# Order of the weight loads in one DMA queue, and place of the last row sums, in a fused attention and soft-MoE kernel

## The chip, the cores and the metric

The kernel runs on one core of one Trainium2 chip. The metric is the device time of one execution in microseconds (us); smaller is better. Times of a profile count from the start of its span.

## The reference

Two stages follow each other. Attention has 4 batches, 8 heads, 768 positions and head dimension 64. Four of the heads ("retrieval") see all earlier positions, the other four only the first 4 positions and a window of 64. Its output is turned into 3072 rows of 512 numbers, the input `x` of a soft mixture of experts with 8 experts of 4 slots:

```python
logits = x @ phi                       # 3072 x 32
d = softmax over the rows of logits    # dispatch, per slot
slot_input = d.T @ x                   # 32 x 512
slot_out[e] = relu(slot_input[e] @ w1[e]) @ w2[e]   # w1: 512 x 1024, w2: 1024 x 512
out = softmax over the slots of logits @ slot_out   # 3072 x 512
```

All inputs and the output are float32 in HBM.

## The kernel before, in words

**Loads.** All large inputs come through one queue, POOL's, which casts float32 to bfloat16 on the way: q, k and v in "quads" of four heads of a batch (8 quads each, `load`, L100), 8 first expert matrices `w1s` and 8 second ones `w2s` (`w_load`, L389 to L394; the last ones in halves of 256 columns, `w2_half`, L396). The order is that of the string `LOADS` (L39): its first six entries are issued at the start, the rest by `issue` (L492), called after each `turn` of a quad. A name such as `v7` may go out only when the quad two before it (`v5`) has been turned, since it is put in the same buffer; a `w` is the next expert matrix and has no such condition. But the list is taken strictly in order, and POOL issues in order. What is left of the first 12 matrices after the list goes out behind the turn of `v6` (`weights(12)`, L521). The buffers of q, k and v and of the masks are those of `w2s[4]` to `w2s[7]`, so these matrices come last: (4), (5) and the first half of (6) behind the last turn of `v7` (L523 to L525), the other three halves (7,0), (6,1), (7,1) after the attention's last mask (L578).

A DMA further waits for the eighth one before it on the same queue: the trace shows POOL's issues from 65.45 us on ended by landings of such loads.

**Attention.** The instruction order of TensorE (PE), ScalarE (ACT) and VectorE (DVE) is written out by hand in `ORDER` (L41): `Tv7.1` turns half of v's quad 7 on PE (L120), `ev7.1` copies it out of PSUM, `Q` are scores (L166), `x` exponentials (L174), `M` masks (L193), `P` the products with v (L208), `N` the division (L220, L222), `X`, `L`, `S`, `B`, `D` the logits, their exponentials and the slot inputs of a finished batch. Each engine runs its part strictly in this order, so PE at a `T` whose quad has not landed holds up all that follows.

**Around the end of the attention.** `expT` holds the exponentials of the logits, one block a batch. `row_sums(b)` (L598) makes the sums over slots of one batch, six matmuls of one column each. For batches 0 to 2 they run ahead of the last slot inputs; for the last batch, at L620, they wait for ScalarE's copy of the last exponentials (`last_turn`, L297). One reciprocal of all 24 sums follows on DVE (L621, `rrow`).

**Experts.** `first(e4, c)` (L637) makes half the hidden units of four experts (16 matmuls of 512 columns into one PSUM bank), `turn_h` transposes them, `second(es, cols)` (L658) multiplies with w2. The expert banks 0 to 7 lie where the attention's PSUM pools were: scores in 0 to 3, two tiles in turn; the tile `tail` in 4 and 5; transposes in 6 and 7. The last two experts come per half of the columns (L729, L733): `slot_out` columns 0 to 255 need halves (6,0) and (7,0), columns 256 to 511 need (6,1) and (7,1).

**Output.** For eight of twelve blocks of 256 rows, the first half of the columns is made and stored as soon as the first half of `slot_out` is there (`half_rows(i, 0)`, 8 stores of 256 KB), then the second half (8 more), then the other four blocks whole (`full_rows`, 4 stores of 512 KB). All 20 stores go through SP's queue in this order (L691). PE, DVE and ACT only feed them.

Of the kernel before, what the change touches and what calls it, by code (L numbers as in the profile page):

```python
# [35 lines left out]

LOADS = "q0 k0 v0 q1 k1 v1 q2 k2 v2 w q3 k3 w v3 q4 k4 w v4 w q5 k5 v5 w q6 k6 w v6 q7 k7 w w v7 w".split()  # L39

ORDER = """  # L41
Tq0.0 Tq0.1 E eq0.0 eq0.1 Y4 Tk0.1 H2.3 H1.2 Tk0.0 H1.1 ek0.1A H0.1 H0.0 ek0.0 H0.2 H0.3 Y4 Q0.1 H1.3 Q0.4
# [31 lines left out]
HP = [0, 1, 2, 3, 4, 5, 6, 7]  # L74
# [255 lines left out]
def kernel(  # L330
# [13 lines left out]
    nc = tc.nc  # L344
    P = 128
    B, H, S, D = q.shape
# [12 lines left out]
    for i, t in enumerate("qkv"):  # L359
        w = w2s[4 + i].rearrange("p f (hp c) -> p (f hp c)", hp=2)  # L360
# [7 lines left out]
    quarter = singles.tile([P, 1], BF16, name="quarter")  # L368
# [3 lines left out]
    rrow = singles.tile([P, B, 6], F32, name="rrow")  # L372
# [115 lines left out]

    queue = LOADS[6:]
    turns = {}  # L490
# [86 lines left out]
    bl = B - 1  # L577
# [4 lines left out]
    tail = unread[0]  # L582
    sip = tail[:, 0, :4 * ES].rearrange("p (o s) -> p o s", o=4)

    def slot_inputs(x, first):
        v = x.rearrange("p (di do) -> p do di", do=4)
        if first:
            nc.tensor.matmul(tail[:, 0, :4 * ES], ident, zero[:, :4 * ES], start=True, stop=False)
        for do in range(4):
            nc.tensor.matmul(sip[:, do, :], v[:, do, :], sum4, start=False,  # L590
                             stop=not first and do == 3)

    def out_rows(b, c, r):
        return expT[:, b, 256 * c + r:256 * c + 256:2]

    rp = tail[:, 1, 448:448 + 6 * B].rearrange("p (b c) -> p b c", b=B)

    def row_sums(b):  # L598
        for c in range(3):
            for r in range(2):  # L600
                nc.tensor.matmul(rp[:, b, 2 * c + r:2 * c + r + 1], out_rows(b, c, r), quarter, start=True, stop=True)

    slot_inputs(slot_sa, True)
    fill(2)
# [3 lines left out]
    at.by_feature(nc.scalar.copy, slot_sl, slice(0, 256), slps[0])  # L608
    at.by_feature(nc.vector.tensor_copy, slot_sl, slice(256, 512), slps[1])
    at.last_exps(bl, True)  # L610
    for b in range(bl):
        row_sums(b)
    slot_inputs(slot_sl, False)
    nc.vector.tensor_copy(siT, sip)
    at.last_turn(bl)
# [1 line left out]
    nc.vector.reduce_sum(csum, colpart, axis=AX.X)  # L617
    rcol = singles.tile([P, 1], F32, name="rcol")
    nc.vector.reciprocal(rcol, csum)
    row_sums(bl)  # L620
    nc.vector.reciprocal(rrow, rp)  # L621
    sctx.close()
    mlp = ctx.enter_context(tc.tile_pool(name="mlp", bufs=2, reuse_waits="tile"))
    osb = ctx.enter_context(tc.tile_pool(name="osb", bufs=12, reuse_waits="tile"))
# [2 lines left out]
    def bank(i, shape, dt=F32):  # L627

        return tps.tile(shape, dt, tag=f"b{i}", name=f"b{i}")
# [7 lines left out]
    def first(e4, c):  # L637
        hp = bank(HP[2 * e4 + c], [P, 512])
        for do in range(4):
            for g in range(4):  # L640
                nc.tensor.matmul(hp[32 * g:32 * (g + 1), :], siT[:, do, :], w1s[4 * e4 + g][:, do, c * 512:(c + 1) * 512],
                                 start=(do == 0), stop=(do == 3))
        if e4 not in hss:
            hss[e4] = mlp.tile([P, 2, 512], BF16, tag="hs", name="hs")
        if c == 0:
            nc.scalar.activation(hss[e4][:, 0], hp, ACT.Relu, scale=emask[:, e4:e4 + 1])
        else:
            nc.vector.tensor_scalar(hss[e4][:, 1], hp, emask[:, e4:e4 + 1], 0.0, op0=ALU.mult, op1=ALU.max)

    def turn_h(e4):  # L650
        tp = bank(HP[4 + e4], [P, 8, P], BF16)
        hv = hss[e4].rearrange("p c f -> p (c f)").rearrange("p (fi fo) -> p fo fi", fo=8)
        for fo in range(8):
            nc.tensor.transpose(tp[:, fo, :], hv[:, fo, :], ident)
        hTs[e4] = mlp.tile([P, 8, P], BF16, tag="hT", name="hT")
        nc.vector.tensor_copy(hTs[e4], tp)
# [15 lines left out]

    first(0, 0)
    first(0, 1)
    first(1, 0)
    turn_h(0)
    first(1, 1)
# [96 lines left out]
```

## Time and profile before

| | |
|---|---|
| time, median of 3 runs | 150.86 us (150.58 to 151.81) |
| the profiled execution | 151.69 us, of which its span 149.9 us |
| busy in the span | PE 124.4, weight loads into PE 83.1, DVE 113.2, ACT 103.8, POOL 35.3 us |
| PE's granted clock, mean | 0.948 |
| HBM read, written | 52.50 MB, 6.29 MB |
| DMA packets | 16838, 32.91 MB |

The span is what the profiler covers; 1.8 us of the profiled execution lie around it. The profile's second part cuts the span in 40 slices of 3.75 us, with a digit for the busy tenths of each engine. An "idle before" in a timeline is the time in which an engine waited ahead of an instruction, with what ended the wait. A DMA has an issue time and a time to landing; the sum of both is when its data can be used. Both are told per load, by the window of its issue.

### The profile page before, as it was taken

The numbers are of one execution on the slowest core, as the hardware profiler recorded it, in microseconds if no ns is written. First come the engines' busy times: TensorE is split into PE (matmuls) and PEld (weight loads), VectorE is DVE, ScalarE is ACT, GpSimd is POOL, SyncE is SP. The second block draws the span as 40 slices with busy tenths as digits, with TensorE's granted clock in tenths as the row PEclk, the third lists the DMA queues.
The fourth block names the chain that finished last, engine by engine and source line by source line (L and its number), as shares of the span: only waits on it lengthen the run. The fifth ranks groups of instructions, "written<-read, shape, count | busy, mean of one in ns | idle before, by whom it ended". The sixth has DMA issues, their size and how long they took to land.

```text
span 149.9 us, 5211 instructions
## 1 busy us (share of the span) xinstructions
PE 124.4 (83%) x2301; PEld 83.1 (55%) x2303; DVE 113.2 (76%) x256; ACT 103.8 (69%) x142; POOL 35.3 (24%) x68
## 2 busy tenths in 40 slices
PE   6899999999999999999999947989879699575000
PEld 2455677677766676658657725556556457451000
DVE  4898999999969999998999973488993343758000
ACT  3049899999899999889989962289931430769000
POOL 6634401603146022337220000064033000000000
PEclk9999999999999999999999995599999999999855
DMA  2999999999999999999999999999999999789995
GB/s 22 197 210 210 211 234 202 215 230 192 227 207 219 204 210 222 207 220 218 199 229 212 211 221 213 214 223 210 214 219 214 192 198 196 159 301 346 345 405 201
DMA packets 16838, 32.91 MB, mean 220 GB/s; under 512 B 1712, under 2 KB 9904, under 8 KB 15024
## 3 DMA queue, kind: packets, MB, share of 16 engines
q0 software_dynamic: 11168, 26.22, 91.3%
q1 hardware_dynamic: 5648, 6.37, 12.4%
q8 instruction: 18, 0.29, 0.7%
q14 instruction: 4, 0.03, 0.1%
HBM read 52.50 MB, written 6.29 MB: 392 GB/s over the span
## 4 chain that ended last, share of the span: by engine, by line
PE 28%; DMA 25%; issue 21%; ACT 11%; POOL 4%; DVE 2%; ACTq 0%; POOLq 0%
DMA w<-in_q_dram 13%; DMA w<-in_moe_w_dram 12%; PE sc L166 8%; PE pv L208 6%; ACT pT L174 6%; PE tpk L120 2%; PE tpv L120 2%; ACT ot L711 2%; PE tpx L231 2%; PE tpq L120 2%; POOL w L397 1%; POOL expT L264 1%; PE tpb L138 1%; PE zp L422 1%; ACT ot L724 1%
## 5 line engine op out<-in xcount | busy, mean ns | idle before, releaser
L174 ACT ACTIVATE pT<-sc 128x1024 bf16<-128x1024 f32 (+1 forms) x96 | 81.3, 930 | 9.3 <-PE sc L166 9.0
L193 DVE TENSOR_TENSOR pT<-pT,w 128x1024 bf16<-128x1024 bf16 (+2 forms) x64 | 32.6, 524 | 3.1 <-ACT pT L174 3.0
L166 PE MATMUL sc<-qT,kT 64*128 64x512 bf16 (+3 forms) x256 | 33.0, 313 | 1.9 <-ACT pT L174 1.3
L208 PEld LDWEIGHTS <-pT 128*128 128x128 bf16 x672 | 25.5, 99 | 9.9 <-issue 7.9
L208 PE MATMUL pv<-vb,pT 128*128 128x65 bf16 x352 | 28.9, 196 | 0.1
L120 PEld LDWEIGHTS <-w 96*64 96x64 bf16 x768 | 18.9, 111 | 12.3 <-issue 6.2
L208 PE MATMUL pv<-vf,pT 128*128 128x65 bf16 x320 | 24.7, 196 | 0.0
L222 DVE TENSOR_TENSOR xb<-pv,rs 128x768 bf16<-128x768 f32 (+1 forms) x17 | 15.5, 910 | 0.6
L166 PEld LDWEIGHTS <-kT 64*128 64x128 bf16 x256 | 10.3, 94 | 9.8 <-issue 3.9
L264 POOL COPY expT<-ep 128x128 bf16<-128x128 bf16 x18 | 6.8, 426 | 22.8 <-ACT ep L260 22.6
L120 PE MATMUL tpv<-ident,w 96*64 96x96 bf16 x256 | 8.6, 213 | 3.1 <-DMA w<-in_v_dram 3.1
L153 DVE TENSOR_TENSOR vf<-vb,fmask 128x528 bf16<-128x528 bf16 x16 | 11.2, 697 | 0.0
L711 ACT ACTIVATE ot<-b,rrow 128x256 f32<-128x256 f32 x16 | 6.0, 489 | 6.9 <-PE b L705 6.9
L132 DVE COPY vT<-tpv 128x768 bf16<-128x768 bf16 x14 | 7.4, 548 | 3.1 <-PE tpv L120 3.1
L236 DVE COPY xT<-tpx 128x768 bf16<-128x768 bf16 x16 | 8.7, 549 | 1.1 <-PE tpx L231 1.1
L103 POOL DMA_DIRECT2D w<-in_k_dram x8 | 5.1, 641 | 17.7 <-PE sc L166 11.6
L231 PE MATMUL tpx<-ident,xb 128*128 128x128 bf16 x96 | 8.3, 224 | 1.0 <-DVE xb L222 0.8
L120 PE MATMUL tpq<-ident,w 96*64 96x96 bf16 x256 | 8.1, 209 | 0.7 <-DMA w<-in_q_dram 0.7
L132 DVE COPY qT<-tpq 128x768 bf16<-128x768 bf16 x15 | 8.0, 548 | 0.6 <-PE tpq L120 0.6
L422 PE MATMUL zp<-w 128*128 128x512 bf16 x21 | 7.3, 480 | 1.3 <-DVE quarter L425 1.2
L120 PE MATMUL tpk<-ident,w 96*64 96x96 bf16 x256 | 8.3, 209 | 0.0
L103 POOL DMA_DIRECT2D w<-in_q_dram x8 | 5.3, 667 | 12.1 <-PE tpq L120 11.2
(106 smaller groups left out, 149.3 us busy)
## 6 DMA issues: line engine op xcount, KB each, us to landing
w<-in_moe_w_dram POOLq DMA_DIRECT2D x14, 1024.0 KB, 21.6
out_dram<-ot SPq DMA_DIRECT2D x16, 256.0 KB, 3.5
w<-in_q_dram POOLq DMA_DIRECT2D x8, 384.0 KB, 15.1
w<-in_k_dram POOLq DMA_DIRECT2D x8, 384.0 KB, 13.8
w<-in_v_dram POOLq DMA_DIRECT2D x8, 384.0 KB, 18.1
w<-in_moe_w_dram POOLq DMA_DIRECT2D x4, 512.0 KB, 17.1
out_dram<-ot SPq DMA_DIRECT2D x4, 512.0 KB, 4.6
phf<-in_moe_phi_dram SPq DMA_DIRECT2D x4, 16.0 KB, 9.3
```

The costliest lines, as they stand in the source:

```text
L103: self.nc.gpsimd.dma_start(self.raws[t][Q % 2][:96], s)
L120: self.nc.tensor.transpose(tp[64 * hp:64 * hp + 64, x, :], raw[:96, hp, s * 64:s * 64 + 64], self.ident[:96, :96])
L132: self.nc.vector.tensor_copy(o, i)
L153: self.nc.vector.tensor_mul(vf, self.vbs[n // 2 % 2][:, n % 2, :, :4, :], fm.to_broadcast([128, 2, 4, VW]))
L166: nc.tensor.matmul(sc[:, hh, o:o + w], kT[ps, (g0 + j) * 128:(g0 + j + 1) * 128], qT[ps, g0 * 128 + q0:g0 * 128 + q0 + w], start=True, sto ...
L174: self.nc.scalar.activation(self.pT[n][:, :, lo:hi], self.sc.pop((n, u))[:, :, :hi - lo], ACT.Exp, scale=self.scale)
L193: nc.vector.tensor_mul(v, v, m)
L208: self.nc.tensor.matmul(pv[:, i * 65:(i + 1) * 65], pT[:, hh, o:o + 128], (vb if i - j <= 1 else vf)[:, j, :65], start=(j == 0), stop=(j = ...
L222: nc.vector.tensor_mul(x[:, hs], pv[:, :, :, :64], rs[:, :c].to_broadcast([128, c, 6, 64]))
L231: self.nc.tensor.transpose(tp[:, i * 128:(i + 1) * 128], self.xb[b][:, i, n4 * 128:(n4 + 1) * 128], self.ident)
L422: nc.tensor.matmul(zp[:, i % 2, :], zw[:, :128], zw, start=True, stop=True)
L711: nc.scalar.activation(o[:, r, :], op[:, r, :], ACT.Copy, scale=rr[:, r:r + 1])
```

## The change

Two edits. The list of loads gets one weight behind each quad of q, k and v from the third quad on, always behind v. Before, some weights stood ahead of v, and there were nine of them; now there are six, and six instead of three are left for `weights(12)`:

```diff
-LOADS = "q0 k0 v0 q1 k1 v1 q2 k2 v2 w q3 k3 w v3 q4 k4 w v4 w q5 k5 v5 w q6 k6 w v6 q7 k7 w w v7 w".split()
+LOADS = "q0 k0 v0 q1 k1 v1 q2 k2 v2 w q3 k3 v3 w q4 k4 v4 w q5 k5 v5 w q6 k6 v6 w q7 k7 v7 w".split()
```

The row sums of the last batch move from ahead of the experts to behind `first(0, 1)`, into expert bank 5. The one reciprocal becomes two, of 18 and of 6 sums, each behind its sums:

```diff
-    rp = tail[:, 1, 448:448 + 6 * B].rearrange("p (b c) -> p b c", b=B)
-
-    def row_sums(b):
-        for c in range(3):
-            for r in range(2):
-                nc.tensor.matmul(rp[:, b, 2 * c + r:2 * c + r + 1], out_rows(b, c, r), quarter, start=True, stop=True)
+    def row_sums(bs, rp):
+        for i, b in enumerate(bs):
+            for c in range(3):
+                for r in range(2):
+                    nc.tensor.matmul(rp[:, i, 2 * c + r:2 * c + r + 1], out_rows(b, c, r), quarter,
+                                     start=True, stop=True)
+        nc.vector.reciprocal(rrow[:, bs[0]:bs[-1] + 1], rp)
...
-    for b in range(bl):
-        row_sums(b)
+    row_sums(range(bl), tail[:, 1, 448:448 + 6 * bl].rearrange("p (b c) -> p b c", b=bl))
...
-    row_sums(bl)
-    nc.vector.reciprocal(rrow, rp)
...
     first(0, 0)
     first(0, 1)
+    row_sums([bl], bank(HP[5], [P, 1, 6]))
     first(1, 0)
```

## The prediction, made before the changed kernel was run

> **What bounds the kernel now.** First the page: slices, queues, then the chain.
>
> ```profile
> PE   6899999999999999999999947989879699575000
> DMA  2999999999999999999999999999999999789995
> GB/s 22 197 210 210 211 234 202 215 230 192 227 207 219 204 210 222 207 220 218 199 229 212 211 221 213 214 223 210 214 219 214 192 198 196 159 301 346 345 405 201
> q0 software_dynamic: 11168, 26.22, 91.3%
> ```
>
> The DMA engines have no gap from 4 to 127 us; POOL's load queue has nearly all of that. Only slices 34 and 35 (127 to 135 us), where loads give way to stores, dip. The chain says the same of the end:
>
> ```profile
> 112.74 18.55 DMA w<-in_moe_w_dram
> 131.28 0.04 issue
> 131.33 0.63 PE b L668 x14
> 131.96 0.02 issue
> 131.98 0.48 ACT slot_out L734
> ```
>
> The last weight half, (7,1), lands at 131.28; outputs and stores follow. An engine is late once, in PE's timeline:
>
> ```profile
> 87.27 0.53 PE L120 MATMUL tpk<-ident,w 96*64 96x96 bf16 x16
> 90.94 0.29 PE L120 MATMUL tpv<-ident,w 96*64 96x96 bf16 x2 [3.14 <-DMA w<-in_v_dram]
> ```
>
> and in the table by stretch (columns: stretch; length; PE, weight loads, DVE, ACT, POOL busy; PE's clock; DMA share; GB/s):
>
> ```profile
> 89.00:90.00 1.00, 0.00 (x0) 0.00 (x0) 0.05 (x1) 0.10 (x1) 0.00 (x0) 1.00 1.09 221
> 90.00:91.00 1.00, 0.06 (x2) 0.06 (x4) 0.00 (x0) 0.00 (x0) 0.00 (x0) 0.52 0.98 205
> 95.00:96.00 1.00, 1.00 (x5) 0.48 (x4) 0.69 (x1) 0.25 (x1) 0.00 (x0) 0.50 1.13 238
> 96.00:97.00 1.00, 1.00 (x12) 0.67 (x11) 0.00 (x0) 0.00 (x0) 0.00 (x0) 0.57 1.02 213
> 128.00:128.50 0.50, 0.50 (x7) 0.45 (x5) 0.30 (x1) 0.08 (x1) 0.00 (x0) 1.00 0.70 95
> 134.00:134.50 0.50, 0.50 (x5) 0.32 (x4) 0.50 (x2) 0.50 (x2) 0.00 (x0) 1.00 0.18 59
> ```
>
> PE waits 3.14 us for v7, and runs at half clock from 90.0 to about 96.9. DMA is as full there as ever. From 127.5 to 130 the loads move 95 GB/s instead of 198: half of the 16 engines have finished, the others need until 130 or 131.
>
> **The change, part by part.** The sum is made against the profiled execution (151.69 us, span 149.9), 0.83 above the median of 150.86; the difference is applied to the median.
>
> *Loads.* v7, issued at 66.98, took 23.9 us: it landed at 90.90. Ahead of it the old list has eight weights, the new five. Weights issued at 73.56, 75.42, 77.26 took 26.7, 29.6, 32.7 us: one lands 4.87 us behind the other. So v7 lands at 90.90 - 3 x 4.87 = 76.3, 11 us before PE comes to it at 87.80. On PE this returns 3.14 us of idling and about half of the 5.9 us run at half clock, 6.1 us together; ACT, idle for 3.28 + 0.82 + 2.38 = 6.5 us between 89 and 98, can follow. The attention ends between 3.1 us (the idle time alone) and 6.1 us earlier; I take 5, nearer the upper end, since PE and ACT are back to back on either side.
>
> What is late next is the load queue. No byte is added or removed, and POOL still issues 18 matrices; the moved ones go out at once behind `S1`'s copies (69.3 to 71.5), bound by the eighth load before. So (6,0), (7,0), (6,1), (7,1) land as before if the queue never runs dry. Tightest is k6: issued at 55.36 when PE has turned k4. Ahead of it q6 landed at 46.66 + 19.7 = 66.4; with one weight less in front 61.5, and 58.9 on the fast engines (2.6 earlier, as 130.2 less 127.6). The first load needed at most 1.5 us from issue to full flow (1.28 to 2.8), so k6 is ready at 56.9: 2 us to spare, cost nothing. If that cover goes, each dry us costs one.
>
> *Row sums.* The experts' first matmul starts at 118.73, behind six row sums that waited 0.99 us for ACT's copy. PE is free of the previous work at 117.50, `siT` is ready at 117.24. The gain is at least 0.23 (the six matmuls), if the bank is held by the tile ACT still reads, at most 1.23; I take 1.2, since two score tiles alternate and by count that tile has the other pair of banks. Back in comes 0.23 us of PE behind `first(0, 1)` and a second reciprocal on DVE, at most 0.31 each (24 columns took that): the first lies in DVE's idle 0.46 ahead of `siT`, the second in the 0.87 ahead of `hT`. Nothing waits for `rrow` before 128. No DMA moves.
>
> *What of it reaches the end.* Some 6 us of compute come forward, but `slot_out` needs (7,0), which lands at 111.00 + 13.96 = 124.96. Before, PE reached its product late (the last 16 matmuls ended near 127.2). Now it waits for the load, idling from about 121.
>
> ```profile
> 127.25 0.48 DVE L730 TENSOR_SCALAR slot_out<-b,rcol 128x256 bf16<-128x256 f32 x1 [1.62 <-PE b L668]
> 128.92 0.61 SPq L691 DMA_DIRECT2D out_dram<-ot  x1
> ```
>
> From slot_out to the first store are 1.67 us, so the store goes at 124.96 + 0.04 + 0.63 (the same product at 131.33) + 0.05 + 1.67 = 127.35, or 127.85 if PE is at half clock (0.3 for the product, 0.2 for the first output). That is 1.1 to 1.6 us before 128.92.
>
> The end follows only in part. Stores run at 346 GB/s (256 KB) and 399 (512 KB): 4.19 / 0.346 + 2.10 / 0.399 = 17.4 us. Half of the engines can start them 1.35 us earlier; the other half have loads until 130.25 and then 17.4 us of stores, to 147.65 instead of 148.1: only the dip at 134.0 (0.45 us) is left to gain there. Bounds 0.45 and 1.35; half the engines being at each, I take the middle, **0.9 us**. The second half's chain allows it: 131.28 to its first ready output at 133.6 (134.1 at half clock), against a store issue at 135.25.
>
> At one place a rule is to be weighed. PE's clock fell 2.2 us into an idle time of 3.14 us, and did not in one of 1.42 us (129.9). The Trainium skill (TensorE: Matmul & The Clock Gate, Part 1) has the clock halved after an idle window of about 3.4 us, free-running; by its length the stall at 87.8 should not have sufficed, and the trace decides. By either, the new wait of over 3 us before 125 costs the 0.5 above.
>
> **Rivals.** *A, nothing reaches the end:* the slower engines set it and the dip at 134 comes back, 0.2 us gained: 150.7. For it: they have work without a gap from 4 us on. Against: half the engines idle for 2 us now.
>
> *B, slower: the early stores hold up the last load.* They reach the engines near 128.6, when the slow half still has 1.65 to 2.7 us of (7,1). Sharing evenly doubles that: it lands at 132.9 to 134.0, and the second half's first store, 2.8 us later at half clock, goes at 135.7 to 136.8 instead of 135.25: +0.45 to +1.55, 151.3 to 152.4. It decides from a landing behind 132.4 on. For it: (7,1) came 3.66 us behind (6,1), which came 2.66 behind (7,0), and stores ran beside it from 130. Against: the trace's packets of the instruction queue show a 16 KB block of 0.97 us on an engine at 127.8, which explains as much. The Trainium skill (DMA: Bandwidth & Descriptors, Queues, rings and completion order) has each engine take turns between queues by packet; that speaks for B.
>
> *C, the queue runs dry* near 59 us: 1 to 3 us lost, 151.9 to 153.9. Against: 2 us to spare.
>
> *D, all follows:* stores 1.6 us earlier on every engine and no dip at 134: -2.0, 148.9. For it: SP issues them one behind the other from the first on.
>
> *E, v7 is no earlier,* because its issue is held: it waited 0.99 us for q6's landing. In the new order the eighth load before it is k5, landed long before; even so, row sums alone free 1.2 of the 1.6 us: 150.2, in the forecast's range.
>
> **How the numbers follow.** Forecast (with E) 0.50, A 0.19, B 0.14, C 0.04, D 0.13. Predicted 150.86 - 0.9 = 150.0; the forecast's own range is 149.3 to 150.5 (gains of 1.6 to 0.4). For 8 in 10 it runs from D's 148.9 to the middle of B's, 151.8. Over 1% faster (below 149.35; 1% is about what a measurement of this kernel can tell from no change): D and a part of the forecast, 0.21. Over 1% slower (above 152.37): the end of B, most of C, 0.09. Within 1%: 0.70.
>
> **What would show it.** Right: no wait for v7 in PE's timeline, its landing near 76, clock 1.00 from 88 to 97; `first` at PE's end of `last_turn`; the weights' DMA share above 0.9 until 127; the product for columns 0 to 255 waiting for a weight near 125; first store at 127.4 to 127.9. Wrong: a DMA share below 0.9 between 56 and 75 (C), (7,1) landing behind 132.4 (B), first store no earlier than 128.5, or last loads landing before 130, which would break the sum, since it takes the load time as fixed.

## The result, and the profile after

| | median | runs | ratio to before, 95% interval |
|---|---|---|---|
| before, beside it | 151.21 us (150.46 to 152.79) | 16 | |
| after | 152.0 us (151.58 to 152.8) | 16 | 1.0061 [1.0037, 1.0085] |

The change makes the kernel 0.4 to 0.9% slower. The forecast was 0.9 us faster; the time lies 0.2 us above the range given. The profiled execution of after took 152.03 us (span 150.3), so it stands for the median; PE's mean clock is 0.945. The times of before fall into two groups (of the 91 in this comparison and those below, 49 lie at 151.01 us or less and 41 at 151.2 or more), and the execution of 151.69 us that the prediction read belongs to the upper one.

First the page of after: the slices of PE, of its clock and of the DMA engines, GB/s, and two queues, the loads' (q0) and the instructions' (q8).

```profile
PE   6799999999999999999999998987989923984000
PEclk9999999999999999999999999999999995699755
DMA  2999999999999999999999999999999999789995
GB/s 25 202 210 209 210 225 208 209 228 201 211 227 200 217 226 196 226 208 206 219 217 227 216 212 212 214 222 216 216 214 212 192 199 193 174 273 345 342 401 202
q0 software_dynamic: 11168, 26.22, 91.0%
q8 instruction: 18, 0.29, 0.7%
```

The clock row of before, for comparison:

```profile
PEclk9999999999999999999999995599999999999855
```

The DMA row is the same digit for digit, so the DMA engines had no new gap. PE's dent has moved from slices 23 and 24 (86 to 94 us) to slices 32 and 33 (120 to 127 us), and half speed in the clock row from slices 24 and 25 to 33 and 34. The last row is of use further down: 18 packets bring 0.29 MB of instructions, 16,384 bytes each. Such a packet is called a block here.

The first half of the forecast came true. The issue of v7, in POOL's timeline, and the answer on its tile:

```profile
66.17 0.63 POOL L103 DMA_DIRECT2D w<-in_v_dram  x1 [2.69 <-PE tpv L120]
...
DMA to landing us min/median/max: 9.5/9.5/9.5
```

v7 landed at 66.17 + 9.5 = 75.7 instead of 90.9, and nothing waits for it. In the table by stretch (columns as in the prediction), the old stall is gone, and a new one stands 30 us later:

```profile
88.00:97.00 9.00, 8.47 (x141) 5.42 (x140) 8.21 (x18) 7.71 (x11) 4.06 (x9) 1.00 1.03 216
...
121.00:122.00 1.00, 0.00 (x0) 0.00 (x0) 0.00 (x0) 0.00 (x0) 0.00 (x0) 1.00 1.44 203
122.00:123.00 1.00, 0.00 (x0) 0.00 (x0) 0.00 (x0) 0.00 (x0) 0.00 (x0) 1.00 1.47 194
123.00:124.00 1.00, 0.38 (x2) 0.10 (x2) 0.00 (x0) 0.00 (x0) 0.00 (x0) 0.74 1.45 199
124.00:125.00 1.00, 0.00 (x0) 0.00 (x0) 0.00 (x0) 0.00 (x0) 0.00 (x0) 0.50 1.45 197
...
126.00:127.00 1.00, 0.95 (x14) 0.52 (x14) 0.01 (x1) 0.00 (x0) 0.00 (x0) 0.50 1.46 198
```

From 88 to 97 us PE now works 8.47 of 9 us at full clock (6.05 us at a mean clock of 0.62 before). From 121 to 126 it does next to nothing, and its clock is halved by 124. PE's timeline says why:

```profile
111.40 0.49 PE L295 MATMUL tpl<-perm,el 128*128 128x128 bf16 x6
111.93 1.91 PE L639 MATMUL b<-w,siT 128*32 128x512 bf16 x32
...
118.23 2.36 PE L666 MATMUL b<-w,hT 128*32 128x256 bf16 x64
123.43 0.38 PE L666 MATMUL b<-w,hT 128*32 128x256 bf16 x2 [2.84 <-DMA w<-in_moe_w_dram]
125.92 1.04 PE L666 MATMUL b<-w,hT 128*32 128x256 bf16 x14 [2.11 <-DMA w<-in_moe_w_dram]
127.53 3.25 PE L704 MATMUL b<-slot_out,expT 128*128 128x256 bf16 x16 [0.58 <-DVE slot_out L729]
```

The experts start at 111.93, 6.8 us earlier than before (118.73), right behind `last_turn`. Then PE waits 2.84 us for (6,0) and 2.11 us for (7,0), and its product with (7,0) and the first outputs run at half clock: 1.04 and 3.25 us. The chain that ended last runs through that load:

```profile
105.35 20.53 DMA w<-in_moe_w_dram
125.88 0.04 issue
125.92 1.05 PE b L666 x11
126.97 0.03 issue
126.99 0.49 DVE slot_out L729
127.49 0.04 issue
127.53 2.73 PE b L704 x12
```

So (7,0) landed at 125.88, where the forecast took 124.96. SP's timeline has the first store:

```profile
128.87 0.60 SPq L690 DMA_DIRECT2D out_dram<-ot  x1
```

It goes at 128.87, where 127.35 to 127.85 was forecast and 128.92 shown of before. All the 6.8 us of PE's lead are lost again at two loads, (6,0) and (7,0), and at half clock.

### The profile page after: what moved, and what is told of

Its sections match the earlier page's. It is cut to its first block, busy times and chain, and to the rows that moved or that the text cites. A ratio compares the mean times of both kernels' runs of the same rounds, so it can differ in the third digit from the quotient of the medians.

```text
span 150.3 us, 5215 instructions
## 1 busy us (share of the span) xinstructions
PE 124.2 (83%) x2301; PEld 82.5 (55%) x2303; DVE 113.4 (75%) x257; ACT 103.8 (69%) x142; POOL 35.0 (23%) x68
## 4 chain that ended last, share of the span: by engine, by line
PE 32%; issue 20%; DMA 17%; ACT 13%; POOL 7%; DVE 2%; ACTq 0%; POOLq 0%
DMA w<-in_moe_w_dram 14%; PE sc L166 9%; PE pv L208 7%; ACT pT L174 7%; DMA w<-in_k_dram 4%; ACT ot L710 3%; PE tpv L120 3%; POOL expT L264 3%; PE tpk L120 2%; PE b L704 2%; PE tpx L231 2%; POOL w L394 2%; PE tpb L138 2%; PE lgs L255 1%; PE tpq L120 1%
## 5 line engine op out<-in xcount | busy, mean ns | idle before, releaser
L166 PE MATMUL sc<-qT,kT 64*128 64x512 bf16 (+3 forms) x256 | 32.5, 309 | 2.0 <-ACT pT L174 1.3
L208 PEld LDWEIGHTS <-pT 128*128 128x128 bf16 x672 | 25.0, 97 | 9.3 <-issue 7.2
L208 PE MATMUL pv<-vb,pT 128*128 128x65 bf16 x352 | 28.3, 194 | 0.1
L666 PE MATMUL b<-w,hT 128*32 128x256 bf16 x128 | 5.7, 290 | 5.2 <-DMA w<-in_moe_w_dram 5.2
```

What stands on the lines that cost most here:

```text
L166: nc.tensor.matmul(sc[:, hh, o:o + w], kT[ps, (g0 + j) * 128:(g0 + j + 1) * 128], qT[ps, g0 * 128 + q0:g0 * 128 + q0 + w], start=True, sto ...
L208: self.nc.tensor.matmul(pv[:, i * 65:(i + 1) * 65], pT[:, hh, o:o + 128], (vb if i - j <= 1 else vf)[:, j, :65], start=(j == 0), stop=(j = ...
```

## The experiments

**The theory.** The first store is set by the landing of (7,0) and by PE's clock there, and the end by the first store. In the quicker executions of the kernel before, PE is already at (7,0) by the time that it lands; then being earlier can gain nothing. The change adds two losses: a PE that is further ahead idles until its clock is halved, and its instructions are fetched sooner, in blocks of 16 KB that go through the same DMA engines as the loads, one of them now ahead of (7,0). The rivals: the slow execution shown of before is the typical one, and the loss is in the load queue's new order itself; or the early stores hold up the last load (B of the prediction), though (7,1) landed at 131.18, as before.

**One edit alone, each.** `loads_only` is the kernel before with the new `LOADS`; `sums_only` is after with the old string, so only the row sums and reciprocals are moved. The edit of `sums_only` against after, the string shortened at its start:

```diff
-LOADS = "... v2 w q3 k3 v3 w q4 k4 v4 w q5 k5 v5 w q6 k6 v6 w q7 k7 v7 w".split()
+LOADS = "... v2 w q3 k3 w v3 q4 k4 w v4 w q5 k5 v5 w q6 k6 w v6 q7 k7 w w v7 w".split()
```

> The new order of loads alone; the row sums stay where they were. Theory T (the end is set by the landing of (7,0) and by PE's product behind it; what the loads free is eaten by a block of instructions that is fetched through a DMA engine ahead of (7,0), 0.9 us, and by PE at half clock, 0.6 us): as the changed kernel, first store at 128.8 to 129.0, about 0.8 us above the kernel before. Rival R (the moved row sums cost it): as the kernel before or faster, 150.4 to 151.2.

> The moved row sums alone; the old order of loads, so PE still waits 3.1 us for v7. T: the experts start 1.2 us earlier, PE stays at full clock, (7,0) lands at 125.0 and the first store goes at 127.6 to 128.0; 0.3 to 1.0 us under the kernel before. Rival R: 0.5 to 0.8 us above the kernel before. Rival D (the DMA engines set the end whenever the first store goes): within 0.2 us of the kernel before.

Measured: `loads_only` 151.73 us, ratio to before 1.0037 [1.0007, 1.0067]; `sums_only` 150.61 us, 0.9989 [0.9957, 1.0021]. The loads' order makes the loss, and the row sums alone can't be told from no change. Each comparison has its own executions of before beside it, so two kernels are best compared by their ratios. Two of the expected first stores were missed: that of `loads_only` goes at 128.42, ahead of 128.8 to 129.0, since the product with (7,0) still ran at full clock, and that of `sums_only` at 127.21, ahead of 127.6 to 128.0. PE's timeline of `loads_only` has the wait for (7,0), and a clock that is full for the product but half for the outputs:

```profile
125.89 0.61 PE L668 MATMUL b<-w,hT 128*32 128x256 bf16 x14 [2.93 <-DMA w<-in_moe_w_dram]
...
127.08 3.31 PE L705 MATMUL b<-slot_out,expT 128*128 128x256 bf16 x16 [0.57 <-DVE slot_out L730]
```

In that of `sums_only` PE waits too, but (7,0) is there 1.0 us sooner, and the clock stays full:

```profile
124.88 0.61 PE L666 MATMUL b<-w,hT 128*32 128x256 bf16 x14 [0.72 <-DMA w<-in_moe_w_dram]
```

Its first store, at 127.21, is 1.66 us ahead of after's. That is where the forecast had wanted it (127.35 at full clock), without the loads' edit.

**256 PE instructions fewer.** If the block of instructions ahead of (7,0) makes it late, a kernel with one block less must have it at the old time although the load order is the new one. `less256` leaves out, in after, four of the six products with v of the last row block of every head, 128 weight loads and 128 matmuls; that part of the attention is then not computed.

```diff
             for j in range(i + 1):
+                if i == 5 and 0 < j < 5:
+                    continue
```

> The changed kernel with 256 PE instructions less, so that one block of instructions less is fetched before the end: it leaves out four of the six products with v of the last row block of every head (128 weight loads and 128 matmuls). T: (7,0) lands at 124.8 to 125.1 instead of 125.88, the first store goes near 128.0, and the time is 0.5 to 1.0 us under the changed kernel. Rival D: the first store goes earlier and the time stays within 0.2 us of the changed kernel's. If the late landing has another cause than the fetch, (7,0) lands at 125.9 as in the changed kernel.

Measured: 150.77 us, 0.9984 [0.996, 1.0008] of before. PE's timeline:

```profile
125.01 1.04 PE L668 MATMUL b<-w,hT 128*32 128x256 bf16 x14 [2.38 <-DMA w<-in_moe_w_dram]
```

(7,0) is there at 124.97, 0.9 us earlier than in after, while PE waits as long and the clock is still halved (1.04). Less work on PE can't have done it directly, since PE was waiting, and the first of the 16 engines ends its part of (7,0) at 122.27 in this run and at 122.24 in after, so the load queue as a whole was not ahead. By the ratios the gain on after is 1.2 us, more than the 0.5 to 1.0 expected. `sums_split`, below, makes the same test the other way round.

**The clock alone, and both.** `warm` fills the wait with products that nothing reads, so that PE keeps its clock; as many products with v are left out elsewhere (22), so that the number of PE instructions stays:

```diff
+                if i == 4 and 0 < j < 3 and hh == 0 and n < 11:
+                    continue
...
     second((4, 5), (0, 1))
+    warm = bank(HP[0], [P, 512])
+    for i in range(22):
+        nc.tensor.matmul(warm, ident, w1s[0][:, 0, :512], start=True, stop=True)
```

`warm_less256` has this and the edit of `less256`.

> The changed kernel with 22 matmuls of 512 columns that nothing reads behind the products of experts 4 and 5, to keep PE's clock up; 22 products with v are left out, so that the number of PE instructions, and with it the block fetched ahead of (7,0), stays. T: (7,0) lands at 125.9 as in the changed kernel, the product takes 0.6 us, the first store goes at 128.1 to 128.4, 0.4 to 0.7 us under the changed kernel. If the clock alone were the cause: 1 us or more under it. If only the fetch were: no change.

> As less256, and with 22 matmuls of 512 columns that nothing reads behind the products of experts 4 and 5, so that PE isn't idle before (7,0); 22 further products with v are left out, so that the number of PE instructions is that of less256. T: PE's clock is 1.00 from 120 to 128, the product takes 0.6 instead of 1.05 us, the first store goes at 127.4 to 127.6, the time is 1.0 to 1.5 us under the changed kernel. Rival D: within 0.2 us of the changed kernel.

Measured: `warm` 151.25 us, 1.0019 [0.9992, 1.0047], by the ratios 0.6 us under after; `warm_less256` 150.92 us, 1.0007 [0.9981, 1.0033]. The profiled execution of `warm` had all loads 2.2 us late, so no line of it is used. Of `warm_b`, the same kernel again, only the distance from the landing to the first store is used: 2.57 us, against 2.99 in after; 0.2 us of it are fills that outlast the load. `warm_less256` was a miss in part: the clock was full (0.62 for the product), but nothing was gained over `less256`, since the fills outlasted the load, and the first store went at 127.87 instead of 127.4 to 127.6. They ended at 125.6 and (7,0) had landed at 124.92:

```profile
125.53 0.62 PE L668 MATMUL b<-w,hT 128*32 128x256 bf16 x16
```

**80 PE instructions more.** In `sums_only` the block in question starts at 125.08, 0.24 us behind the landing of (7,0). If the theory holds, a few more PE instructions bring it ahead, and (7,0) comes late with the old load order. `sums_split` cuts each fill product (`fill`, unread) of `sums_only` in six, 80 instructions more in all:

```diff
-            nc.tensor.matmul(unread[0][:, 1, :448], ident, w1s[0][:, 0, :448], start=True, stop=True)
+            for k in range(6):
+                nc.tensor.matmul(unread[0][:, 1, 74 * k:74 * k + 74], ident, w1s[0][:, 0, 74 * k:74 * k + 74],
+                                 start=True, stop=True)
```

> As sums_only, with the 8 unread filling matmuls of 448 columns near the end of the attention each cut into 6 of 74 (80 PE instructions more, the same columns). The block of instructions that came at 125.08 in sums_only, just behind the landing of (7,0), is then due some 2 us earlier, ahead of it. T: it comes at 123 to 124, (7,0) lands at 125.7 to 125.9 instead of 124.84, the first store goes near 128.1 instead of 127.21, and the time is 0.6 to 1.2 us above sums_only. If the fetch doesn't matter: (7,0) at 124.8 and within 0.3 us of sums_only.

Measured: 151.16 us, 1.0012 [0.9987, 1.0038]: over `sums_only` by 0.55 us in the medians and 0.35 by the ratios, whose intervals overlap, and under the 0.6 to 1.2 expected. The landing is clearer than the time. PE's timeline:

```profile
126.01 0.61 PE L668 MATMUL b<-w,hT 128*32 128x256 bf16 x14 [0.48 <-DMA w<-in_moe_w_dram]
```

The block starts at 122.80 and (7,0) lands at 125.97 instead of 124.84. So a block less brings (7,0) forward, and a block ahead of it puts it back, each seen in one profiled execution. The new order by itself is not the cause: (7,0) is on time with it in `less256`, and late with the old order in `sums_split`. Where the delay sits can be read from the landings of (7,0) and (6,0), which the trace has in 16 parts, one for each DMA engine, but without the engine's name. About half of the engines finish within 1.2 us of the first, the others 1.4 to 3.8 us behind it; here the last eight, in us behind the first engine:

```
             block starts   (6,0), the last eight engines       (7,0), the last eight engines
before_b       124.90       2.5 2.5 2.6 2.6 2.6 2.7 2.8 2.9     2.5 2.5 2.6 2.6 2.6 2.6 2.8 2.9
after          121.16       2.3 2.3 2.4 2.4 2.5 2.5 2.5 3.8     2.3 2.3 2.4 2.4 2.5 2.5 2.5 3.6
less256        120.93       1.4 2.4 2.4 2.5 2.5 2.5 2.6 2.7     2.4 2.4 2.4 2.4 2.5 2.5 2.6 2.7
```

In after one engine alone is a good 1 us behind the rest, and it stays so for the last loads; a load has landed when its last engine is through. That the blocks put it there can be followed through the whole trace of after. The load that lands at 11.7 us, ahead of the first block (13.36), ends on all 16 engines within 0.6 us. Behind eight blocks (the load that lands at 60.4) eight engines are 1.0 to 1.2 us late, behind sixteen (at 119.5) eight are 2.3 to 2.6 us late, and behind the 17th one of these is 3.8 us late. So each block costs one engine about 1 us that it does not make up, and the blocks go round eight of the engines: their durations (0.975, 0.961, 0.893, 0.892, 0.948, 0.945, 0.935, 0.974 us for the ninth to the 16th) are those of the first eight to 0.001 us, in the same order. The 17th is the third on its engine. In `less256` the block near 121 is the 16th: it moves the one engine that stood at 1.4 to 2.4, level with the others, and the load is no later for it. The Trainium skill (Runtime: NRT & Kernel Launch, Instruction fetch mechanics) says that the sequencer refills instructions in blocks of 16 KiB, 256 instructions, through a DMA queue of its own, and calls the cost mostly hidden. The size agrees (18 packets of 16,384 bytes); hidden it is not where a load is the bound: 0.9 to 1.1 us in the two pairs of runs.

**The kernel before, again.** The second question is what a usual execution of the kernel before looks like.

> The kernel before once more, whose times lie in two groups, near 150.5 and near 151.5 us; for the trace of another execution. T: the end stands 18.9 us behind the first store plus what SP loses at one store, so a quicker execution shows an earlier first store or a shorter stop of SP, by its whole difference.

> As before_a, another execution of the kernel before: the same is expected.

Measured: profiled executions of 151.01 and 150.59 us, against the 151.69 shown ahead of the prediction; the medians of before in the four comparisons lie at 150.7 to 151.21. PE's products with the last weights in the execution `before`, where no wait stands ahead of them:

```profile
124.83 2.37 PE L668 MATMUL b<-w,hT 128*32 128x256 bf16 x80
```

The same in `before_a`:

```profile
123.55 2.37 PE L668 MATMUL b<-w,hT 128*32 128x256 bf16 x80
```

PE's timeline of `before_b`:

```profile
90.62 0.53 PE L120 MATMUL tpv<-ident,w 96*64 96x96 bf16 x16 [1.59 <-DMA w<-in_v_dram]
...
125.20 0.61 PE L668 MATMUL b<-w,hT 128*32 128x256 bf16 x14 [1.26 <-DMA w<-in_moe_w_dram]
126.39 1.91 PE L705 MATMUL b<-slot_out,expT 128*128 128x256 bf16 x16 [0.58 <-DVE slot_out L730]
```

and its stretch from 88 to 97 us:

```profile
88.00:97.00 9.00, 6.98 (x134) 4.67 (x132) 7.36 (x16) 6.09 (x9) 1.33 (x4) 1.00 1.05 217
```

v7 lands as before (its product starts at 90.62, against 90.94), but PE comes to it later, waits only 1.59 us, and its clock is not halved. It is then early enough at (7,0) to wait there 1.26 us, with no edit at all, and the first store goes at 127.52. In `before_a`, with a wait of 2.24 us for v7 and a mean clock of 0.81 there, PE's last 14 products, those with (7,0), begin some 0.6 us before 125.92, when it has just landed (125.25), and the first store goes at 127.64. In the execution `before` they begin near 126.6, 1.6 us behind the landing.

**Both good halves together, and after again.** `sums_less256` is `sums_only` with the edit of `less256`.

> The moved row sums with the old order of loads, and 256 PE instructions less (four of the six products with v of the last row block of every head are left out). T: one block of instructions less reaches the engine that lands last, so (7,0) lands at 124.8 to 125.0 and (7,1) at 130.3 instead of 131.2; the ninth store, which stood behind (7,1) at 133.8 in sums_only, goes at 133.0 to 133.4; 0.3 to 0.7 us under sums_only's 150.61. If the stores are the limit by themselves: within 0.2 us of sums_only.

> The kernel warm once more, for the trace of an execution in which the loads land on time. T: (7,0) at 125.9, the product behind it at full clock in 0.6 us, the first store at 128.1 to 128.4 against 128.87 in the changed kernel.

> The changed kernel once more, another execution. T: the fetched block ahead of (7,0) again, (7,0) at 125.7 to 126.0, the product at half clock, the first store at 128.6 to 129.0.

Measured: `sums_less256` 150.7 us, 0.998 [0.995, 1.0011]; its (7,0) landed at 126.0, where 124.8 to 125.0 was expected, and its (7,1) at 131.29 instead of 130.3. That is a miss: one DMA engine ran some 3.4 us behind from 86 us on in this execution. Two of its engines were 1.6 us late at 12.7 us already, ahead of the first block (14.24), and two blocks on top of that would come to such a lag; but the landings don't tell which engine is which, so the cause is not settled. `warm_b` took 152.23 us, with its whole load stream 0.8 us late, so that its (7,0) and first store missed what was expected, and `after_a` 151.79, with (7,0) at 126.00: like after.

All profiled executions but that of `warm` (the starts of the blocks and the landings are from the trace's records; us):

| kernel | 17th block, with `less256`'s edit 16th | (7,0) landed | first store | last store landed | profiled time |
|---|---|---|---|---|---|
| before | 127.79 | 124.96 | 128.92 | 148.57 | 151.69 |
| before_a | 126.51 | 125.25 | 127.64 | 147.85 | 151.01 |
| before_b | 124.90 | 125.16 | 127.52 | 147.43 | 150.59 |
| sums_only | 125.08 | 124.84 | 127.21 | 147.36 | 150.49 |
| sums_split | 122.80 | 125.97 | 128.34 | 148.09 | 151.21 |
| loads_only | 122.81 | 125.85 | 128.42 | 148.35 | 151.48 |
| after | 121.16 | 125.88 | 128.87 | 148.90 | 152.03 |
| after_a | 122.29 | 126.00 | 129.00 | 148.66 | 151.79 |
| less256 | 120.93 | 124.97 | 127.97 | 147.47 | 150.59 |
| warm_less256 | 120.74 | 124.92 | 127.87 | 147.81 | 150.93 |
| sums_less256 | 124.95 | 126.00 | 128.37 | 148.04 | 151.17 |
| warm_b | 123.05 | 126.42 | 128.99 | 149.07 | 152.23 |

Three things can be read from it. Where a kernel that leaves nothing out has the 17th block at 122.81 or earlier, (7,0) lands at 125.85 or later; where the block comes at 124.90 or later, at 124.84 to 125.25. The first store goes 2.36 or 2.37 us behind the landing at full clock (before_b, sums_only, sums_split) and 2.99 or 3.00 at half clock (after, after_a, less256), if PE is waiting. And the last store lands 19.5 to 20.2 us behind the first store's issue in all twelve.

## Why the prediction was wrong, step by step

**v7, the clock and the attention: right.** v7 landed at 75.7 (76.3 forecast), the wait is gone, and the clock is 1.00 from 88 to 97. The first fill products of the last stage (L487 in both) come 5.65 us earlier, at 106.94 instead of 112.59, inside the 3.1 to 6.1 and near the 5 taken.

**The load queue never dry: right**, by the DMA row and by the first engine of the sixth-last load (done at 112.06 us, against 112.09 in before).

**The row sums: right**, 1.15 of the 6.8 us, with 1.2 taken.

**"(6,0), (7,0), (6,1), (7,1) land as before": failed** for the first two. (7,0) came at 125.88, 0.92 later than the step had it, because a block of instructions met one engine ahead of it. That is nearly all of the miss at the first store, which went at 128.87 where 127.85 was forecast for half clock. (7,1) landed at 131.18, as forecast: in before, the block lay between the landings of the two. The prediction had seen such a block at 127.8 and used it to explain the late (7,1), but took its place in time as fixed. It isn't: blocks are fetched as PE moves on, and PE was made 6.8 us earlier.

**Half clock at the product: right in kind, too small.** 0.5 us was taken; 2.99 - 2.36 = 0.63 was measured. A second product waits too, for (6,0), which the prediction didn't split off.

**The room at the first store: failed for the quicker executions.** 128.92 was taken as the first store of the kernel before, and the gain of 1.1 to 1.6 us counted from there, then subtracted from a median that was 0.83 us below that execution. There PE came late to (7,0), after a longer stall and a longer stretch of half clock at v7 than in the other two. In before_a and before_b the first store goes at 127.64 and 127.52, and in before_b PE already waits for (7,0). Against these the forecast's own first store, 127.35 at full clock and 127.85 at half, leaves a gain of 0.2 to 0.3 us or a loss of 0.2 to 0.3. Against before_b the sum now closes: (7,0) 0.72 us later, clock 0.63, first store 128.87 - 127.52 = 1.35 later; last store landed 148.90 - 147.43 = 1.47 later; profiled time 1.44 longer. Against the execution `before`, the first store goes 0.05 us earlier and the time is still 0.34 longer. By the medians it is 0.79 longer, since the executions of before vary. So two steps failed: the landing of (7,0), by 0.6 to 0.9 us against all three executions of before, and the room, by 1.3 to 1.4 us against the two quicker ones.

**"The end follows only in part": near in size, only in part for its reason.** The three earliest first stores of the table (before_a, before_b, sums_only) go 1.28, 1.40 and 1.71 us ahead of that of the execution `before`, and their last stores land 0.72, 1.14 and 1.21 us earlier; the step took 0.9 for 1.1 to 1.6. But one or two engines, not eight, are behind at the end there: the last of the 16 ends its part of the last store 0.75, 0.40 and 0.72 us behind the first, while in the other nine executions all 16 end within 0.25 us. With the other pairs the end moves by more or less than the first store: from after to less256 by 1.43 for 0.90 us, from sums_only to sums_split by 0.73 for 1.13. A stop of 0.5 to 1.1 us in SP's issuing (below) makes much of that, and in before_b and sums_only a wait of the ninth store, the first of the second half, for its output (0.73 and 0.35 us in SP's issue records): there (7,1) has become the limit. The dip at 134 that the sum counted as left to gain comes right behind such a stop in before (one issue from 132.32 to 133.83), and no execution of the table was without one. The sum's 148.1 for the end of before was low, too; the last store landed at 148.57.

**The rivals.** B is refuted, though not by after, whose first store was no earlier than in before: in before_b and sums_only the first stores went at 127.52 and 127.21, and (7,1) still landed at 131.26 and 131.23, not behind 132.4. C didn't occur, nor E. A, that nothing reaches the end, has the right number for the row sums alone (0.9989, interval with 1 in it); its reason, slower engines at the end, is seen in part (the 0.72 us above). D, that the end follows in full, gives too much: 0.6 to 0.8 of it in the three executions named above. No rival had PE's own lead as the harm.

**What stays open.** Which event starts the last block of instructions, at 128.9 to 132.3, isn't known (it comes 45 to 164 PE instructions behind the one ahead of it, the others mostly 200 to 400), nor why one engine fell behind in `sums_less256`, nor why PE's arrival at v7 varies by over 1 us between executions of the same kernel. No complete version was clearly better than before: `sums_only` is 0.7% under after by the ratios, and not to be told from before.

## What to carry to other kernels

Before slack found in a profiled execution is subtracted from a median, look whether that execution stands for the median: here the slack of 1.1 to 1.6 us belonged to one execution, 0.83 us above the median, and two others of the same kernel had 0.3 us or less of it. Where the loads are back to back to the end, a stall taken out of an engine ahead of them can come out again at the last load that its results need; ask what the engine does while it waits there (here its clock halved and its next instructions were fetched sooner), since that can make the change a loss. The chain of stores that one queue issued back to back followed its first store to within 0.7 us, so the first store's own condition was what to price.

## What the runs showed of the hardware

- A block of PE instructions occupied one DMA engine for 0.89 to 0.98 us in after (the first 17 blocks), and with the load queue full that engine stayed about 1 us behind: each later load landed that much later where this engine was the last one.
- In after SP's issue of the stores stops at such a block. Its timeline has two issues, 0.60 us each else, that last 2.33 us together; one of them took 1.66, to 131.85, and the last block ran from 129.92 to 131.44. In every execution of the table one issue is held like this, and ends 0.4 to 0.7 us behind the last block; that the block holds it is not shown. The lines of after:

```profile
129.52 2.33 SPq L690 DMA_DIRECT2D out_dram<-ot  x2
```

- PE's clock fell at 123.5, 2.9 us behind PE's last long stretch of work, which ended at 120.6, and came back at 130.3. Of the waits for v7, 1.59 us (before_b) left it full, while 2.24 (before_a) and 3.14 us (before) didn't. The Trainium skill (TensorE: Matmul & The Clock Gate, Part 1) names about 3.4 us of idle window; none of these waits was that long. The clock records of all the traces explain it: every stretch at one clock but the last of a trace is a whole multiple of 3.41 us long (3.41, 6.83, 10.24 and so on), so the clock is set in steps of 3.41 us. In 28 of 29 falls PE's matmuls had covered 0.41 or less of the step before (the exception, in loads_only: 0.73), and the clock stayed full behind every step with 0.47 or more but that one. A wait shorter than a step can thus halve the clock, if most of it falls into one step, and the clock may fall when the wait is over: in before_a at 91.59, when PE had been at work again since 90.78.
